# Twelve products of a zero tile ahead of the first transposes in a fused sliding-window attention and mixture-of-experts kernel

## The chip, the cores and the metric

The kernel runs on one core of one Trainium2 chip. The metric is the time of one execution on the device in microseconds (us), given as the median of several runs. The engines are named as the profile names them: PE is TensorE (PEld its weight loads), DVE is VectorE, ACT is ScalarE, POOL is GpSimd, SP is SyncE.

## The reference

Attention in a causal window of 64 positions over 8 batches, 8 heads, 576 positions and 64 channels a head; then the mean over the positions of a batch chooses one of eight experts for the whole batch, and that expert's two layers are applied.

```python
scores = (q @ k^T) / sqrt(64)                       # (8, 8, 576, 576)
mask   = (0 <= i - j) and (i - j < 64)
x      = softmax(where(mask, scores, -1e9)) @ v     # heads side by side: (8, 576, 512)
pooled = x.mean(axis=1)
logits = pooled @ w_gate                            # (8, 8)
e      = argmax(logits);  gate = softmax(logits)[e]
out[b] = gate[b] * (relu(x[b] @ w1[e[b]]) @ w2[e[b]])   # 512 -> 1024 -> 512
```

## The kernel before, in words

A batch is cut into five units: four for two heads each (512 positions), and one for the last 64 positions of all eight heads. The units are numbered through, so unit 0 to 4 are batch 0, 5 to 9 batch 1. For each unit PE transposes q and k (`T`, L225; L232 for the tail unit), ACT or DVE copy the transposes out of PSUM (`k` for the k half, L252, `U` for the q half, L242), PE makes the scores (`S`, L275, for some units with a mask product ahead, L269), ACT takes the exponential (`E`, L288 and L291), DVE or the mask product applies the band (`K`, L297), PE sums the rows by a product with ones (`l`, L309) and multiplies with v (`A`, L331), ACT makes the reciprocal as a logarithm and an exponential (`n`, L351, and `R`, L357), and DVE scales and adds up for the gate (`X`, L364). Before a batch's v can be used, DVE shifts half of it across the partitions (`V`, L150 and L151). When all five units of a batch are through, the gate is worked out (`g j G H I`), POOL reads the chosen expert's number (`P`), and the expert's weights are loaded by that number (`W`, L423 and L426). The experts' products (`c`, L461, L470, L503, L512) follow, mixed with the attention of later batches.

Nothing here is ordered by a scheduler. The table `OPS` at the head of the file is a list of such steps, and each engine gets its instructions in the order of that list and takes them strictly one after the other. An `m` in a step's name puts its result into one of the three buffers `mo` of the PSUM pool `ps_m`, in turn. Loads of q, k (`Q`, L110), the tail rows (`t`, L133), v (`L`, L141 and L145) and weights are issued by POOL; two loads at the start (`Y`, L119) are issued by SP in float32 and cast on DVE (`Cd`, L128).

The list already has a rule for a step `F` that the table before doesn't use, and the tile `warm` of zeros that `F` reads is cleared by DVE's first instruction (L168):

```python
elif c == "F":
    wps = ps_m.tile([128, 512], FP32, tag="mo", name="wps")
    for _ in range(int(x)):
        nc.tensor.matmul(out=wps, lhsT=warm[:, 0:128], rhs=warm, start=True, stop=True)
```

The table's beginning is the loads of batch 0 (`Y0.24 Q0.48 Q1.48 Q0.2 ...`), the casts, and then the transposes of batch 0 in the order unit 3, 2, 0, 1 (`Tm3 Tm2 T0 Tm1`), the scores of unit 3 (`Sb3`), and so on. On PE the transposes of unit 3 are the first work of the program.

Of the kernel before, what the change touches and what calls it, by code (L numbers as in the profile page):

```python
# [1 line left out]
OPS = (  # L2
    "Y0.24 Q0.48 Q1.48 Q0.2 Cd0.24 y i Q1.2 Y1.24 Q3 Cd1.24 z Tm3 Tm2 mb T0 Tm1 ka3 ka2 ka0 "
    "t0 Ud3 Ud2 Q2 Sb3 L0 L3 ka1 L1 L2 E3 Smb2 L4 Ud0 l3 Ud1 t1 S0 T4 E2 kd4 Ud4 n3 Smb1 E0 "
    "Mb K0 E1 R3 Q4 L9 Tm5 Sb4 Tm7 Tm8 Ud5 Q5 ka5 kd8 E4 L5 kd7 l1 n1 T6 l4 n4 Ud7 l2 Sb5 ka6 "
    "n2 R1 R4 l0 V0 A3 Ud6 L7 Am1 n0 E5 T9 X3 Am2 Ud9 S7 R2 L8 E7 Ud8 X1 R0 l5 X2 L6 n5 Smb6 "
    "A0 Am4 K7 ka9 E6 t2 X4 X0 Sb8 l7 g0 n7 T12 j0 Q6 Sm9 Tm10 G0 Ud12 kd12 E8 Ud10 H0 E9 "
    "Tm13 Tm11 R7 K9 l6 R5 ka10 Sb12 Ud11 ka13 V1 n6 Q7 l8 P0 Ud13 W0 I0 kd11 T14 Am5 A7 X7 "
    "A6 Ud14 kd14 L12 n8 X5 E12 R6 l12 n12 Sm14 X6 S11 l9 E14 Smb10 Tm17 E11 n9 T18 W1 Ud17 "
    "A9 W2 E10 S13 kd18 Ud18 L13 Tm15 Ud15 l10 Am8 R8 W3 kd15 ka17 T16 K14 L11 c X8 L14 n10 "  # L10
    "E13 R9 c ra X9 c R10 c rd c g1 K11 rd S17 j1 G1 ra ra c H1 L10 c rd l14 K13 c t3 ra c P1 "
    "n14 Q8 ra c c rd c V2 Ua16 c c ra ka16 l11 A10 X10 Am12 W4 c Q9 R12 X12 n11 ra W5 R11 "
    "A11 rd W6 T19 E17 c l13 n13 R13 Ua19 I1 X11 c Sm18 S15 K17 L15 rd E18 W7 R14 A13 c l17 "
    "ra X13 A14 c L16 L17 X14 g2 n17 Tm20 E15 ra kd19 c Ud20 ra L18 kd20 T22 S19 Sm16 E19 L19 "
    "j2 G2 c P2 t4 K15 E16 Q10 K18 c ra c W8 H2 ra ka22 c ra c c S20 l18 ra rd rd K16 c n18 "
    "Q11 K19 L21 ra Tm21 c c Ua21 Ud22 l16 W9 T23 R17 kd21 L23 V3 c c R18 c ra Am17 Ud23 n16 "
    "ra l15 E20 X17 L22 c R16 ka23 c rd n15 A18 c S23 X18 Sm21 K20 T24 kd24 ra R15 E21 L20 "
    "A16 c l19 L29 ra L24 W10 n19 Ud24 Am15 X16 A19 W11 R19 c X15 l20 E23 n20 L25 I2 c X19 rd "
    "L26 ra Tm26 c g3 K23 kd26 l23 Ud26 R20 c ra Sm22 n23 S24 j3 rd G3 E24 E22 T28 H3 K21 c "
    "Tm27 Ud28 P3 t5 ka27 kd28 l21 L28 rd n21 I3 K24 S26 L27 T25 c V4 W12 c Ua27 ra l24 c K22 "  # L20
    "c ra ra ra Ud25 n24 c R23 Q13 Q12 Am20 X20 R21 c c c rd Am23 W13 kd25 E26 A21 T29 rd X23 "
    "l22 Sm27 W14 W15 n22 E27 S28 V5 c c K26 K27 L32 c R24 l26 c X21 t6 A24 E28 Am22 ra R22 "
    "L30 ra K28 n26 X24 Ud29 kd29 c A27 l27 n27 c X22 ra ra c g4 S25 R26 rd Sm29 j4 G4 L34 "
    "E29 T32 Tm30 kd30 E25 Ud30 c Ua32 H4 K29 P4 ka32 ra c l28 R27 T33 L33 rd Ua33 S30 I4 n28 "
    "c Q15 c ra L31 ra Am26 ka33 c E30 c ra W16 X27 X26 ra l29 c K25 R28 c rd n29 Q14 A28 K30 "
    "c W17 X28 T34 S32 Sm33 ra O O E32 c E33 c K32 l25 n25 R25 c kd34 Am25 A29 W18 c O Ua34 "
    "R29 rd W19 T31 l30 c X29 X25 rd ka31 g5 c c Ud31 O ra K33 rd Sm31 n30 S34 j5 G5 c V6 R30 "
    "P5 rd O E31 H5 c K31 T36 l32 Ud36 rd E34 c t7 c A30 c n32 I5 rd L39 ka36 ra R32 l33 T35 "
    "X30 A32 Ua35 L38 rd c K34 rd c ka35 c n33 T37 ra Sm35 S36 L37 O E35 rd c X32 ra E36 W20 "
    "l34 c L35 n34 c K35 K36 L36 c kd37 R33 c O l31 rd W21 R34 rd c n31 R31 c Ua37 Tm38 O W23 "  # L30
    "Ud38 A33 ra ka38 Am34 l35 T39 X33 c n35 W22 c ra X34 A31 X31 g6 kd39 c O Sm38 R35 O S37 "
    "ra E38 j6 c c G6 P6 Ud39 E37 ra ra c V7 K38 rd H6 c l36 c K37 W24 n36 S39 A35 l37 ra rd "
    "E39 c ra n37 c X35 R36 c A37 c ra l38 Am36 K39 ra c c O R37 rd X37 n38 Am39 X36 O c rd c "
    "I6 l39 W27 R38 c n39 O O A38 rd R39 c W25 W26 ra X39 X38 g7 c j7 O c G7 c ra c P7 rd ra "
    "c c O W29 O c ra c O rd H7 O ra c O c W28 W31 ra O ra O c ra c c ra rd c c c c rd c W30 "
    "I7 O ra O c rd c c ra rd O c O O rd c O rd O O c rd c c O ra c c rd c O rd ra rd c c O "
    "rd O c c ra O O c c c c ra rd o O c ra O c ra o "
).split()

# [554 lines left out]
```

## Time and profile before

| | |
|---|---|
| median of 3 runs | 203.21 us |
| lowest and highest | 202.68 and 203.79 us |
| span of the profiled execution | 201.9 us, from its first to its last instruction |
| PE busy | 183.5 us (91% of the span) |
| ACT, DVE, POOL busy | 131.8, 119.9 and 111.0 us |
| bytes moved by DMA | 41.16 MB, mean 204 GB/s |

The span leaves out what lies around the first and the last instruction. Which of the three runs the profile was taken in isn't recorded; the span is 0.8 to 1.9 us below them, and 1.3 us below their median. "L225" is a line of the kernel before; in the changed kernel the table is one line shorter, so every line has a number lower by one there.

### The profile page before, as it was taken

How to read it: one execution, taken by the hardware profiler on the slowest of the kernel's cores; microseconds unless marked ns; L12 is line 12 of the kernel's file. 1: busy time of each engine (PE TensorE's matmuls, PEld its weight loads, DVE VectorE, ACT ScalarE, POOL GpSimd, SP SyncE). 2: the span in 40 equal slices, each digit the busy share in tenths (PEclk: the TensorE clock that was granted, in tenths of full speed). 3: DMA queues.
4: the chain of work that ended last, by engine and by line, in shares of the span. 5: the costliest groups of instructions: out<-in, count | busy, mean ns of one | idle time of the engine just before them, and what ended most of it. 6: DMA issues, size and time to landing. Idle time of an engine off the chain costs nothing.

```text
span 201.9 us, 8105 instructions
## 1 busy us (share of the span) xinstructions
PE 183.5 (91%) x3518; PEld 124.2 (62%) x3522; DVE 119.9 (59%) x347; ACT 131.8 (65%) x247; POOL 111.0 (55%) x158
## 2 busy tenths in 40 slices
PE   0487886899999999999999999999999999999991
PEld 0455564656677756577667666676656666776760
DVE  3527989595477546895877457966494651216410
ACT  2179998876599578977779975757787436321121
POOL 7985939235931593478633552439452716553561
PEclk9999999999999999999999999999999999999998
DMA  6999999999999999999999999999999999999693
GB/s 135 175 188 159 194 162 198 199 198 174 196 201 197 170 198 193 174 201 167 200 206 200 169 195 223 259 208 137 183 237 243 266 254 212 274 212 301 235 325 134
DMA packets 83346, 41.16 MB, mean 204 GB/s; under 512 B 48080, under 2 KB 80976, under 8 KB 83312
## 3 DMA queue, kind: packets, MB, share of 16 engines
q0 software_dynamic: 81936, 39.72, 138.5%
q1 hardware_dynamic: 768, 0.85, 1.3%
q8 instruction: 27, 0.44, 0.8%
q10 hardware_dynamic: 608, 0.08, 0.2%
q14 instruction: 7, 0.06, 0.1%
HBM read 61.88 MB, written 9.44 MB: 353 GB/s over the span
## 4 chain that ended last, share of the span: by engine, by line
PE 77%; DMA 9%; POOL 7%; issue 3%; DVE 2%; ACT 1%; POOLq 0%; DVEq 0%; ACTq 0%
PE ph L461 28%; PE po L503 25%; DMA vw<-in_v_dram 9%; PE tp L225 5%; PE ph L470 4%; PE s L275 4%; PE av L331 3%; PE po L512 3%; PE lb L309 3%; POOL vw L141 2%; POOL km L110 2%; POOL qm L110 1%; POOL out_dram L492 1%; PE gps L392 1%; POOL qkt L133 1%
## 5 line engine op out<-in xcount | busy, mean ns | idle before, releaser
L503 PE MATMUL po<-w2b,hm 128*64 128x512 f16 x512 | 60.1, 379 | 0.0
L461 PE MATMUL ph<-xm,w1b 128*64 128x512 f16 x512 | 60.0, 379 | 0.0
L461 PEld LDWEIGHTS <-w1b 128*64 128x64 f16 x512 | 31.7, 110 | 18.7 <-issue 0.4
L503 PEld LDWEIGHTS <-hm 128*64 128x64 f16 x512 | 30.1, 110 | 19.3
L141 POOL DMA_DIRECT2D vw<-in_v_dram x32 | 28.9, 910 | 13.3 <-DMA w1b<-in_moe_w_dram 4.3
L446 ACT ACTIVATE hm<-ph,gw 128x512 f16<-128x512 f32 x39 | 26.6, 693 | 13.4 <-PE ph L461 13.3
L492 POOL DMA_DIRECT2D out_dram<-ob x31 | 17.2, 557 | 25.0 <-DMA w1b<-in_moe_w_dram 7.0
L351 ACT ACTIVATE ln<-lb 128x512 f32<-128x512 f32 (+1 forms) x40 | 22.5, 563 | 11.8 <-PE lb L309 8.6
L364 DVE CUSTOM_DVE_ANT_0 xm<-av,rl 128x512 f16<-128x512 f32 x32 | 21.6, 686 | 10.4 <-PE av L331 9.5
L482 ACT COPY ob<-po 128x512 f32<-128x512 f32 x18 | 10.6, 586 | 23.6 <-PE po L503 23.6
L448 DVE TENSOR_SCALAR hm<-ph,gw 128x512 f16<-128x512 f32 x25 | 18.7, 748 | 12.1 <-PE ph L461 11.6
L357 ACT ACTIVATE rl<-ln 128x512 f32<-128x512 f32 (+1 forms) x40 | 23.3, 594 | 1.5 <-DVE pool L364 1.3
L225 PE MATMUL tp<-ident,qm 128*64 128x128 bf16 x256 | 13.8, 232 | 7.4 <-DMA qm<-in_q_dram 6.9
L288 ACT ACTIVATE pe<-s 128x1024 f16<-128x1024 f32 x19 | 19.5, 1028 | 1.4 <-PE s L275 0.7
L297 DVE TENSOR_TENSOR pe<-pe,mask 128x1024 f16<-128x1024 f16 x24 | 16.3, 687 | 3.9 <-ACT pe L288 3.1
L252 ACT COPY kT<-tp 128x512 bf16<-128x512 bf16 x19 | 11.2, 597 | 9.0 <-PE tp L225 8.0
L225 PEld LDWEIGHTS <-qm 128*64 128x64 bf16 x256 | 10.7, 118 | 10.0 <-DMA qm<-in_q_dram 6.9
L482 DVE COPY ob<-po 128x512 f32<-128x512 f32 x14 | 9.7, 690 | 10.7 <-PE po L503 10.5
L423 POOL DMA_DIRECT2D w1b<-in_moe_w_dram x16 | 12.6, 785 | 5.9 <-DMA vw<-in_v_dram 2.9
L275 PEld LDWEIGHTS <-kT 64*128 64x128 bf16 x576 | 10.1, 95 | 8.9 <-issue 5.6
L331 PEld LDWEIGHTS <-vw 128*64 128x64 f16 x512 | 12.4, 112 | 4.7 <-issue 1.2
L225 PE MATMUL tp<-ident,km 128*64 128x128 bf16 x256 | 13.9, 231 | 1.4 <-DMA km<-in_k_dram 0.9
(80 smaller groups left out, 267.2 us busy)
## 6 DMA issues: line engine op xcount, KB each, us to landing
w1b<-in_moe_w_dram POOLq DMA_DIRECT2D x16, 512.0 KB, 9.3
w2b<-in_moe_w_dram POOLq DMA_DIRECT2D x16, 512.0 KB, 13.4
out_dram<-ob POOLq DMA_DIRECT2D x31, 256.0 KB, 8.1
vw<-in_v_dram POOLq DMA_DIRECT2D x32, 128.0 KB, 9.0
km<-in_k_dram POOLq DMA_DIRECT2D x7, 512.0 KB, 9.3
qm<-in_q_dram POOLq DMA_DIRECT2D x7, 512.0 KB, 9.0
out_dram<-obt POOLq DMA_DIRECT2D x14, 64.0 KB, 7.7
qkt<-in_q_dram POOLq DMA_DIRECT2D x8, 64.0 KB, 7.6
```

Of the source, the lines that this page charges most:

```text
L141: nc.gpsimd.dma_start(out=vt[:, 2 * J + 1], in_=v[b, :, 128 * J:128 * J + 128].rearrange("h c d -> c h d"))
L225: nc.tensor.transpose(tp[p0:p0 + 64, n, r], t[:, 2 * i + hh, ts(r, 64)], ident)
L288: nc.scalar.activation(out=po, in_=sp[0], func=AF.Exp, scale=scale)
L351: nc.scalar.activation(out=ln, in_=lb[:, 0:n], func=AF.Ln)
L357: nc.scalar.activation(out=rl, in_=lns.pop((b, i)), func=AF.Exp, scale=-1.0)
L364: nc.vector.tensor_tensor_reduce(out=xm[:, i], in0=av.rearrange("q r p -> q (r p)"), in1=rl, scale=1.0, scalar=0.0, op0=ALU.mult, op1=ALU.add,
L446: nc.scalar.activation(out=o, in_=i, func=AF.Relu, scale=g)
L448: nc.vector.tensor_scalar(out=o, in0=i, scalar1=g, scalar2=0.0, op0=ALU.mult, op1=ALU.max)
L461: nc.tensor.matmul(out=ph[64 * c:64 * c + 64], lhsT=w1t[:, kb, ts(2 * ft + c, 64)], rhs=xm[:, kb], start=(kb == 0), stop=(kb == 3), skip_g ...
L482: copy(e)(out=ob, in_=po)
L492: (nc.scalar if n and eng is nc.sync else eng).dma_start(out=dst, in_=src)
L503: nc.tensor.matmul(out=po[64 * c:64 * c + 64], lhsT=hm[:, fb, ts(2 * r + c, 64)], rhs=w2t[:, fb], start=(fb == 0), stop=(fb == 7), skip_gr ...
```

## The change

One word is put at the head of the table, and the rest of the table is only broken into lines differently. PE gets 24 instructions more (twelve weight loads and twelve products of 128x128 by 128x512 zeros, all into one PSUM buffer) ahead of the first transposes. The products are read by nobody. They take one of the three `mo` buffers first, so that every later user of that pool gets the next buffer in turn.

```diff
 OPS = (
-    "Y0.24 Q0.48 Q1.48 Q0.2 Cd0.24 y i Q1.2 Y1.24 Q3 Cd1.24 z Tm3 Tm2 mb T0 Tm1 ka3 ka2 ka0 "
+    "F12 Y0.24 Q0.48 Q1.48 Q0.2 Cd0.24 y i Q1.2 Y1.24 Q3 Cd1.24 z Tm3 Tm2 mb T0 Tm1 ka3 ka2 ka0 "
...
```

The head of PE's queue before: `qm` is the q of batch 0 in SBUF, `tp` the PSUM tile of unit 3's transposes.

```order
L589 UNCONDITIONAL_BRANCH [waits barrier_Pool_Activation_PE_DVE_SP_release]
L225 LDWEIGHTS qm_126 [waits DMASW0_49]
L225 MATMUL tp_146<-ident_105,qm_126 64x128 [waits Pool_49]
```

And now, where ten further pairs like the one shown stand at the line of dots; `warm` is the zero tile, `wps` the buffer that the products go to:

```order
L588 UNCONDITIONAL_BRANCH [waits barrier_Pool_Activation_PE_DVE_SP_release]
L548 LDWEIGHTS warm_110 [waits DVE_49]
L548 MATMUL wps_124<-warm_110 128x512
...
L224 LDWEIGHTS qm_139 [waits DMASW0_49]
L224 MATMUL tp_159<-ident_105,qm_139 64x128 [waits Pool_49]
```

The first transposes still wait for the load of q and for POOL's identity, and now stand behind the products, which wait for DVE's clearing of `warm`. The second place is unit 1's transposes on PE, before:

```order
L225 MATMUL tp_184<-ident_105,km_128 64x128
L225 LDWEIGHTS qm_126 [waits DVE_49]
L225 MATMUL tp_201<-ident_105,qm_126 64x128
```

and now:

```order
L224 MATMUL tp_197<-ident_105,km_141 64x128
L224 LDWEIGHTS qm_139 [waits DVE_49]
L224 MATMUL tp_214<-ident_105,qm_139 64x128 [waits PE_49]
```

Unit 1 is the third to take an `mo` buffer before, and the fourth now; it gets the buffer of the zero products and so has a wait for PE's own earlier work. DVE, ACT, POOL and SP have the same instructions in the same order with the same waits as before, and so has PE outside these two places.

67 rows, old and new, of the table OPS are left out of this document.

## The prediction

> **What bounds the kernel now.** I read the page first, then busy time by stage, then the chain that ended last in order of time, then PE's first instructions one by one.
>
> ```profile
> span 201.9 us, 8105 instructions
> ```
>
> The busy times by stage (us, then busy time of PE, PEld, DVE, ACT, POOL with counts, granted clock, DMA share, GB/s):
>
> ```profile
> 12.50:22.26 9.76, 7.88 (x181) 5.03 (x183) 5.87 (x13) 8.82 (x17) 6.93 (x9) 1.00 1.94 176
> 22.26:31.32 9.06, 7.53 (x210) 5.43 (x212) 7.64 (x32) 8.88 (x19) 5.73 (x8) 1.00 1.95 176
> ...
> 41.00:197.60 156.60, 156.50 (x2838) 104.57 (x2832) 94.15 (x268) 101.97 (x193) 80.94 (x115) 1.00 1.40 213
> ```
>
> From 41 us on PE has no gaps (156.50 of 156.60), so the end is the moment at which PE gets there plus a fixed amount of PE work. Everything turns on the first 41 us, where PE waits. What it waits for there, the chain in order of time says (start, duration, what):
>
> ```profile
> 9.54 9.13 DMA vw<-in_v_dram
> ...
> 18.96 0.89 POOL km L110
> 19.84 2.83 POOL vw L141 x3
> 22.68 8.52 DMA vw<-in_v_dram
> ...
> 31.32 0.88 DVE vw L150
> ...
> 34.09 0.60 DVE xm L364
> ...
> 34.75 0.44 PE av L331 x16
> ...
> 38.18 0.50 issue
> ...
> 41.01 4.32 PE ph L461 x40
> ```
>
> PE first appears at 34.75, and the experts' products begin at 41.01. Before that the chain is a load of batch 0's v that must land before POOL may issue more, the issues and the loads of batch 1's v, and then DVE's shift of that v and what is queued behind it on DVE. None of these steps waits for PE.
>
> **The change, part by part.** First what the change could save. PE's early instructions (start, duration, and in brackets idle time before and what ended it):
>
> ```profile
> 6.88 0.64 PE L225 MATMUL tp<-ident,qm 128*64 128x128 bf16 x8 [6.88 <-DMA qm<-in_q_dram]
> 8.41 0.64 PE L225 MATMUL tp<-ident,km 128*64 128x128 bf16 x8 [0.89 <-DMA km<-in_k_dram]
> 8.83 0.64 PE L225 MATMUL tp<-ident,qm 128*64 128x128 bf16 x8
> ...
> 10.97 0.64 PE L225 MATMUL tp<-ident,km 128*64 128x128 bf16 x8
> 11.54 0.61 PE L269 MATMUL s<-maskb,ident 128*128 128x512 bf16 x1
> ...
> 12.86 0.60 PE L269 MATMUL s<-maskb,ident 128*128 128x512 bf16 x2
> ...
> 17.30 0.39 PE L225 MATMUL tp<-ident,km 128*64 128x128 bf16 x8
> 17.53 0.39 PE L225 MATMUL tp<-ident,qm 128*64 128x128 bf16 x8
> ...
> 20.72 0.38 PE L269 MATMUL s<-maskb,ident 128*128 128x512 bf16 x1 [0.16 <-issue]
> ```
>
> Until about 12.5 us PE runs at half speed: from 8.83 to 10.97 five groups of eight transposes take 2.14 us, 0.43 a group, where at 17.30 a group takes 0.23; the same 128x512 mask product takes 0.61 at 11.54 and 0.38 at 20.72. At 12.86 two of them take 0.60 together, which is full speed already. The column of the granted clock reads 1.00 throughout, so the clock's state must be read here from durations. The products of zeros would put this slow stretch into the idle time ahead of 6.88.
>
> *Their own cost.* They wait for DVE's first instruction:
>
> ```profile
> 1.05 0.27 DVE L168 MEMSET warm<- 128x256 uint32 x1 [1.05 <-PEq L578]
> ```
>
> That is done at 1.32; I start them at 1.4. A 128x512 product lasts 0.61 at half speed and 0.38 at full, 0.23 less; if half speed doubles the spacing from one product to the next, that spacing is 0.23 at full and 0.46 at half speed. The transposes, two at a time and 128 wide, give 0.43 / 4 x 4 = 0.43 for the same 512 columns. I take 0.43: 12 x 0.43 = 5.2, done by 6.6, ahead of q's arrival at 6.88: cost nothing. At worst each takes its full 0.61 with no overlap: 12 x 0.61 = 7.3, done at 8.7. Then unit 3's transposes start late, but all 64 at the fast pace (8 x 0.23 = 1.84) end at 10.5 against 11.4 (10.97 + 0.43) before: still no loss. The added wait in unit 1 is for PE's own finished products and costs nothing; queued behind it is all the rest of PE's work, but it comes after 48 transposes, when the products are long done.
>
> *What it saves at the place.* Before, unbroken work began at 8.41, and the clock rose between 11.97 (11.54 + 0.43, where unit 3's second mask product begins) and 12.86: 3.6 to 4.5 us later. From 1.4 that is 5.0 to 5.9, so the clock is up before 8.41. From 8.41, seven groups at 0.23 in place of 0.43 save 1.4 us, and the two mask products of unit 3 another 0.46: 1.86. Part of it is lost at once, to a load of k for heads 0 and 1 (issue on POOL, and the row of its landing: KB, us from issue to landing):
>
> ```profile
> 4.75 1.63 POOL L110 DMA_DIRECT2D km<-in_k_dram  x2
> km<-in_k_dram POOLq DMA_DIRECT2D x1, 128.0 KB, 4.9
> ```
>
> It lands at 4.75 + 4.9 = 9.65, and unit 0's k transposes would be due at 8.41 + 4 x 0.23 = 9.33: 0.3 lost. So the first scores, and with them the first exponential on ACT, come 1.5 us earlier:
>
> ```profile
> 12.97 1.02 ACT L288 ACTIVATE pe<-s 128x1024 f16<-128x1024 f32 x1 [0.73 <-PE s L275]
> ...
> 19.72 0.38 ACT L351 ACTIVATE ln<-lb 128x256 f32<-128x256 f32 x1 [0.39 <-PE lb L314]
> ```
>
> The start at 12.97 becomes about 11.4.
>
> *Where it goes.* Three later places don't move, since they wait for loads whose issue on POOL has nothing to do with PE:
>
> ```profile
> 7.79 0.90 POOL L110 DMA_DIRECT2D qm<-in_q_dram  x1
> qm<-in_q_dram POOLq DMA_DIRECT2D x1, 512.0 KB, 8.0
> ...
> 15.94 0.41 PE L225 MATMUL tp<-ident,qm 128*64 128x128 bf16 x8
> ...
> 20.34 0.89 DVE L150 COPY vw<-vw 64x2048 f16<-64x2048 f16 x1 [0.54 <-DMA vw<-in_v_dram]
> 22.26 0.63 PE L331 MATMUL av<-pe,vw 128*64 128x64 f16 x28 [0.42 <-DVE vw L151]
> 30.76 0.42 DVE L242 COPY qt<-tp 128x512 bf16<-128x512 bf16 x1 [0.30 <-PE tp L225]
> ```
>
> First, batch 1's q lands at 7.79 + 8.0 = 15.79, and PE now begins its transposes at 15.94, behind the scores of batch 0. PE comes there 1.5 us earlier, waits, and everything behind in its queue is ahead by 0.15 us. ACT, which from 12.97 to the gap ahead of 19.72 was behind its orders, has worked off its backlog by then, and the row sums and logarithms around 20, where PE and ACT take turns, come some 0.4 us earlier (the size of ACT's gap at 19.72 is my measure for that). Second, DVE's shift of batch 0's v already waited 0.54 us for its load at 20.34, and PE's products with v waited for the shift at 22.26: both stay where they are, and what is left is ACT's lead of 0.4. It goes through the rest of batch 0 to its gate and to the issue of its weights. Third, batch 1's v lands at 22.68 + 8.52 = 31.20, and DVE, which ends its copy before it at 30.76 + 0.42 = 31.18, starts the shift at 31.32. DVE earlier by 0.4 waits for the landing instead: at best the shift starts 0.1 earlier. Behind it DVE has no gap up to 34.69, and PE's next product with v stands on that (34.75). So of the 1.5 us, 1.35 end at 15.94, the 0.4 that ACT wins back end at 31.32, and at 34.75 the kernel is 0 to 0.1 us earlier; I take 0.1. What PE has to do from there is unchanged. 24 more instructions shift where PE's code is fetched; the 0.5 us at 38.18 that the chain puts down to "issue" is my bound for that, 0.5 either way. So the cost of the whole change lies between 1.86 gained and, with the worst rival below, 1.4 lost.
>
> The sum against the profiled span: 201.9 - 0.1 = 201.8, and against the median 203.21 - 0.1 = 203.1.
>
> **The rivals.**
>
> *The lead is carried.* If the landing at 31.20 moves with the rest, or DVE's shift is not what PE's product at 34.75 stands on, PE's lead of 1.5 us lives. It can't be worth more than 1.86, and the chunk at 41 needs its weights: first half issued at 30.04, landing 9.4 us after it.
>
> ```profile
> 30.04 0.75 POOL L423 DMA_DIRECT2D w1b<-in_moe_w_dram  x1 [1.34 <-DVE kT L252]
> w1b<-in_moe_w_dram POOLq DMA_DIRECT2D x1, 512.0 KB, 9.4
> ```
>
> That is 39.4, a margin of 1.6 to the start at 41.01. I take 1.2, so that something of the 1.5 is lost to other loads: 202.0 us. For it: a changed pace of DVE could shift POOL's issues and with them landings that come of a chain of issues. Against it: three waits for loads in a row, the last with 0.14 us of slack.
>
> *The clock falls back.* The twelve products end at 6.6 or sooner, and the next products that aren't transposes are the masks at about 10.1. If transposes don't hold the clock, PE is again at half speed when the scores come, and stays so in the stretch 12.5 to 22.26, which it crosses with pauses while it waits for loads. The end of the program shows how long the clock holds without work:
>
> ```profile
> 180.00:201.90 21.90, 17.61 (x234) 12.58 (x230) 6.42 (x10) 4.09 (x7) 8.63 (x16) 0.96 0.81 252
> 196.54 1.07 PE L512 MATMUL po<-w2b,ht 128*64 128x256 f16 x16
> ```
>
> A mean of 0.96 over 21.9 us means half speed for some 1.75 us, from 200.1, that is 2.5 us after PE's last product ends (197.61). From 6.6 to 10.1 is 3.5 us, longer than that. The price, from PE's work in the stretch 12.5 to 22.26 (count, then busy us, mean ns):
>
> ```profile
> L309 PE MATMUL lb<-pe,ones 128*64 128x512 f16 x8 | 1.6, 390 | 0.7 <-ACT ln L351 0.5 <-ACT pe L288 0.2
> L269 PE MATMUL s<-maskb,ident 128*128 128x512 bf16 x5 | 1.6, 383 | 0.2 <-issue 0.2
> L225 PE MATMUL tp<-ident,km 128*64 128x128 bf16 x32 | 1.6, 219 | 0.0
> ```
>
> With q's there are 64 transposes, eight groups at 0.20 more; five mask products and four pairs of row sums at 0.23 more: 1.6 + 2.1 = 3.7. Less the idle 1.9 of that stretch and the lead of 1.5 this is 0.3 at 22.26. The next stretch, with 1.5 idle and no lead, would lose 3.7 - 1.5 = 2.2 if the clock stayed down through it; I take half: 0.3 + 1.1 = 1.4, 204.6 us. The deciding point is whether eight transposes a group count as work. The Trainium skill, "TensorE: Matmul & The Clock Gate", Part 4, says that they don't count as busy in the same way and that full speed doesn't engage for them, which would give this rival's time. Against it stands the trace: the clock rose at about 12.5 after 3.1 us of transposes and only 0.9 us of other products, and held through the groups at 17.30 and 17.53.
>
> *It doesn't do what it says.* The clock isn't up by 8.41, because its window falls badly or zeros don't count: 203.2 us, as before.
>
> **How the numbers follow.** About 0.5% (1.0 us) is what a measurement of this kernel can tell from no change. Forecast, hidden behind the loads: 0.58, 203.1, its own range 202.5 to 203.8 (the 0.5 us of code fetch and the spread of runs). Carried: 0.23, 202.0. Falls back: 0.13, 204.6. Does nothing: 0.06, 203.2. Faster by over 0.5% is the carried case, 0.23; slower the fallen clock, 0.13; the two others, 0.64, lie within. The range of 201.7 to 204.5 takes in most of the carried case and cuts the upper half of the slow one, so that no more than 2 in 10 is left out.
>
> **What would show it.** Right: groups of eight transposes at 0.23 from 8.41, the first exponential near 11.4, PE waiting for a load ahead of batch 1's transposes at 15.8, a longer wait of DVE for v at 20.3 and a new one at 31.2, PE's product with v within 0.1 of 34.75. Wrong: that product a microsecond earlier (the lead is carried), or durations of 0.6 for a mask product after 12.5 (the clock fell).

## The result and the profile after

| | before | changed |
|---|---|---|
| median | 203.53 us (15 runs, 202.68 to 204.46) | 204.45 us (15 runs, 203.64 to 206.27) |
| profiled execution | span 201.9 | time 204.17, span 202.6 |
| ratio | | 1.0063, 95% interval 1.0042 to 1.0085 |

The change makes the kernel slower, by 0.6% in the ratio and by 0.9 us between the medians, where I had forecast no change. In the experiments below every ratio is to runs of the kernel before on the same chip. One profile there, that of the kernel with batch 1's q moved ahead, is of a disturbed run, and only the place of a wait is read from it.

The page of the changed kernel gives the span, with 24 instructions more than before:

```profile
span 202.6 us, 8129 instructions
```

The busy times by stage (us, then PE, PEld, DVE, ACT, POOL with counts, granted clock, DMA share, GB/s):

```profile
8.41:12.50 4.09, 3.73 (x74) 3.03 (x74) 1.27 (x3) 2.34 (x4) 3.83 (x5) 0.58 1.62 183
12.50:22.26 9.76, 7.50 (x165) 4.63 (x165) 5.75 (x12) 8.65 (x16) 7.42 (x10) 1.00 1.92 175
...
41.00:197.60 156.60, 156.47 (x2844) 105.46 (x2840) 94.88 (x268) 102.03 (x193) 80.51 (x115) 1.00 1.39 212
```

From 41 us on PE is as full as before (156.47 of 156.60, before 156.50). But in the first row the clock is 0.58: PE was at half speed in most of the stretch that the products were to have made fast. The early rows say when (start, duration, what, idle time before and its end):

```profile
1.38 4.67 PE L548 MATMUL wps<-warm 128*128 128x512 bf16 x12 [1.38 <-DVE warm L167]
...
6.95 0.41 PE L224 MATMUL tp<-ident,qm 128*64 128x128 bf16 x8 [0.90 <-DMA qm<-in_q_dram]
...
8.53 0.49 PE L224 MATMUL tp<-ident,qm 128*64 128x128 bf16 x8
8.81 0.64 PE L224 MATMUL tp<-ident,km 128*64 128x128 bf16 x8
9.24 0.64 PE L224 MATMUL tp<-ident,qm 128*64 128x128 bf16 x8
...
12.51 1.02 ACT L287 ACTIVATE pe<-s 128x1024 f16<-128x1024 f32 x1 [0.73 <-PE s L274]
```

The products run from 1.38 to 6.05, and groups are fast at 6.95 and 8.29. Then the spacing is 0.43 again (8.81 to 9.24). By the trace's record of the granted clock it rose at 5.3, fell at 8.7 and rose again at 12.1 (before: once, at 12.57). The first exponential starts at 12.51, only 0.46 ahead of before. Further on:

```profile
16.66 0.41 PE L224 MATMUL tp<-ident,qm 128*64 128x128 bf16 x8 [1.10 <-DMA qm<-in_q_dram]
...
22.65 0.63 PE L330 MATMUL av<-pe,vw 128*64 128x64 f16 x28 [0.43 <-DVE vw L150]
...
31.15 0.42 DVE L241 COPY qt<-tp 128x512 bf16<-128x512 bf16 x1 [0.31 <-PE tp L224]
31.61 0.97 DVE L149 COPY vw<-vw 64x2048 f16<-64x2048 f16 x1
...
35.14 0.44 PE L330 MATMUL av<-pe,vw 128*64 128x64 f16 x16 [1.08 <-DVE pool L363]
```

Batch 1's transposes start at 16.66 instead of 15.94, after a wait of 1.10 us for q; the products with v at 22.65 instead of 22.26; PE's place in the chain at 35.14 instead of 34.75. The shift of batch 1's v (31.61, before 31.32) doesn't wait for its load here: it follows a copy that waits for PE's transposes, so PE's lateness goes through. The issue of that q, and the row of its landing:

```profile
7.83 0.90 POOL L109 DMA_DIRECT2D qm<-in_q_dram  x1
qm<-in_q_dram POOLq DMA_DIRECT2D x1, 512.0 KB, 8.8
```

It is issued 0.04 us later than before and takes 8.8 us instead of 8.0. So PE is 0.39 us late at 22 us. The rest comes late: set against the same instructions of before, PE's weight loads are 0.41 us late from 40 to 85 us, 0.48 at 95, 0.65 from 125 to the end.

### The profile page after: what moved, and what is told of

It is laid out like the page before. It is cut to its first block, busy times and chain, and to the rows that moved or that the text cites. A ratio compares the mean times of both kernels' runs of the same rounds, so it can differ in the third digit from the quotient of the medians.

```text
span 202.6 us, 8129 instructions
## 1 busy us (share of the span) xinstructions
PE 187.7 (93%) x3530; PEld 126.2 (62%) x3534; DVE 120.5 (60%) x347; ACT 132.0 (65%) x247; POOL 110.9 (55%) x158
## 4 chain that ended last, share of the span: by engine, by line
PE 66%; DMA 13%; POOL 6%; issue 5%; DVE 4%; ACT 3%; POOLq 1%; DVEq 0%; ACTq 0%
PE ph L460 21%; PE po L502 20%; PE tp L224 6%; DMA w2b<-in_moe_w_dram 5%; DMA w1b<-in_moe_w_dram 5%; DMA qm<-in_q_dram 4%; PE s L274 4%; PE av L330 4%; PE ph L469 3%; PE lb L308 3%; POOL out_dram L491 3%; PE po L511 2%; DVE xm L363 1%; POOL km L109 1%; ACT ln L350 1%
## 5 line engine op out<-in xcount | busy, mean ns | idle before, releaser
L502 PEld LDWEIGHTS <-hm 128*64 128x64 f16 x512 | 31.2, 110 | 18.7 <-issue 0.3
L350 ACT ACTIVATE ln<-lb 128x512 f32<-128x512 f32 (+1 forms) x40 | 22.4, 561 | 12.5 <-PE lb L308 9.2
L447 DVE TENSOR_SCALAR hm<-ph,gw 128x512 f16<-128x512 f32 x25 | 18.7, 748 | 12.1 <-PE ph L460 11.6
L422 POOL DMA_DIRECT2D w1b<-in_moe_w_dram x16 | 12.5, 779 | 6.1 <-DVE kT L251 2.3
L241 DVE COPY qt<-tp 128x512 bf16<-128x512 bf16 x25 | 10.4, 417 | 9.0 <-PE tp L224 5.1
```

The costliest lines, as they stand in the source:

```text
L350: nc.scalar.activation(out=ln, in_=lb[:, 0:n], func=AF.Ln)
L502: nc.tensor.matmul(out=po[64 * c:64 * c + 64], lhsT=hm[:, fb, ts(2 * r + c, 64)], rhs=w2t[:, fb], start=(fb == 0), stop=(fb == 7), skip_gr ...
```

## The experiments

Four theories stand in the expectations. A, B and C come from comparing the two traces and from the first runs; D was formed after the eighth run.

- **A, an early code load.** PE's code comes by DMA in blocks of 16,384 bytes. The 24 added instructions bring the first such load ahead of the landing of batch 1's q, which then lands some 0.8 us later.
- **B, the products' work**, or the clock's fall after it.
- **C, the lead turns idle.** PE, early, waits ahead of batch 1's transposes, and the clock falls in that wait.
- **D, block ends.** PE stands still at every 256th instruction until the next block is there. Added instructions move the block ends to other places of the program, and where a block has gone by quickly, in short instructions, the wait is longer.

The code loads are rows of the DMA queue "instruction" in short windows, 14.0 to 15.2 us of the changed kernel first, then 16.2 to 17.0 us of the kernel before (packets, MB, share):

```profile
q8 instruction: 1, 0.02, 5.0%
```

```profile
q8 instruction: 1, 0.02, 7.5%
```

Both kernels have 27 such loads. The first starts at 14.53 in the changed kernel and at 16.44 before, where it comes behind the landing of q (7.79 + 8.0 = 15.8).

### Work or count: twelve empty products, six, eighteen

`n12_narrow` keeps the count and takes the work away:

```diff
-nc.tensor.matmul(out=wps, lhsT=warm[:, 0:128], rhs=warm, start=True, stop=True)
+nc.tensor.matmul(out=wps[:, 0:64], lhsT=warm[:, 0:128], rhs=warm[:, 0:64], start=True, stop=True)
```

> The twelve products are kept, but 64 columns wide in place of 512, so that PE gets the same 24 instructions and almost no work from them. Theory A (code load): the 24 instructions move PE's first code load (16,384 bytes on one DMA engine, at 16.44 us before and at 14.53 in the changed kernel) ahead of the landing of batch 1's q, which then lands 0.8 us later; so here too the code load comes near 14.5, batch 1's transposes start near 16.6 (15.94 before, 16.66 changed), and the time is like the changed kernel's, 0.3 to 0.7% above before. Theory B (the products' work or the clock's fall that follows it): no work and no early clock here, so the time is as before within 0.15%, and batch 1's transposes start at 15.9.

Measured: 204.69 us, ratio 1.0048 (1.0022 to 1.0075). The loss is there without the work, which can't be its main part. In its profile, the slowest of the twelve runs, the first code load comes at 14.77, and PE waits for q:

```profile
16.86 0.42 PE L224 MATMUL tp<-ident,qm 128*64 128x128 bf16 x8 [1.94 <-DMA qm<-in_q_dram]
```

That is as A has it; but the clock, up at 10.32, also fell from 17.14 to 20.56, as C has it. How much the fall takes can be read from the runs' mean granted clock: 3.4 us at half speed make 0.992 of a span of 203 us. Seven of the twelve runs have 0.997 or more, so no such fall, and their median is 204.34, where before's runs of 0.996 or more have 203.67: most of the loss is there without it.

`f6` and `f18` change the number alone:

```diff
-    "F12 Y0.24 ...
+    "F6 Y0.24 ...
```

> Six wide products in place of twelve: 12 instructions, work from 1.4 to about 4.0 us. Theory A: all or nothing, by whether the code load is asked for ahead of PE's wait for batch 1's q: near 14.5 us and +0.3 to 0.7%, or near 16.4 us and the time as before. Theory B: about half of the excess, +0.3%, wherever the code load is.

Measured: 204.12 us, 1.0041 (1.0013 to 1.0069). The first code load comes at 15.77, between A's two cases and ahead of q, which lands at 16.5 (7.85 + 8.7).

```diff
-    "F12 Y0.24 ...
+    "F18 Y0.24 ...
```

> Eighteen products: PE works past 6.9 us, so that the stretch in which the clock fell in the changed kernel (5.4 to 8.8 us, mostly idle) is mostly filled. Both theories expect the clock to hold: groups of eight transposes at 0.23 us from 8.3, first exponential near 11.2. Theory A: the code load is early all the same, batch 1's transposes start near 16.6, and the time stays 0.3 to 0.7% above before. Theory B (the clock's fall costs): at least as fast as before.

Measured: 206.56 us, 1.0133 (1.0097 to 1.0168), the largest loss so far. In this profile the early clock held, so that PE came to batch 1's transposes still earlier, and waited (12 to 21.5 us):

```profile
16.41 0.41 PE L224 MATMUL tp<-ident,qm 128*64 128x128 bf16 x8 [1.92 <-DMA qm<-in_q_dram]
...
17.63 0.64 PE L224 MATMUL tp<-ident,qm 128*64 128x128 bf16 x8
18.05 0.64 PE L224 MATMUL tp<-ident,km 128*64 128x128 bf16 x8
```

After 1.92 us of idle time the groups are at 0.42 again: the clock fell at 17.33, as C has it.

### Batch 1's q issued earlier

```diff
-    "t0 Ud3 Ud2 Q2 Sb3 ...
+    "Q2 t0 Ud3 Ud2 Sb3 ...
```

> The changed kernel, with the load of batch 1's q issued on POOL ahead of batch 0's tail rows (near 6.4 us in place of 7.8). Theory A: even with the code load on top it lands by about 15.2, PE is no longer late at batch 1's transposes (15.5 in place of 16.66), the 0.39 us at PE's later product with v goes, and the time is 0.2 to 0.4% below the changed kernel's, near before. Theory B: no change against the changed kernel, +0.6%.

Measured: 207.33 us, 1.0162 (1.0121 to 1.0204): a miss. The 512 KB went ahead of the small load of the tail rows, on which PE stands next:

```profile
17.51 0.64 PE L231 MATMUL tpt<-ident,qkt 128*64 128x128 bf16 x8 [2.05 <-DMA qkt<-in_k_dram]
```

It says nothing of A or C, since it made a wait of its own.

### The wait filled, or taken by other work

`f18_fill` puts eight products into the wait that `f18` showed, `f12_fill` four into that of the changed kernel:

```diff
-    "F12 Y0.24 ...
+    "F18 Y0.24 ...
...
-    "K0 E1 R3 Q4 L9 Tm5 ...
+    "K0 E1 R3 Q4 L9 F8 Tm5 ...
```

> Eighteen products at the start, and eight more directly ahead of batch 1's transposes, where PE idled 1.92 us in the kernel with eighteen alone (14.49 to 16.41) and the clock fell from 17.33 to 20.74. Theory C (the lead becomes an idle stretch ahead of that late load, and the clock falls in it): with the stretch filled the clock holds, groups of eight transposes stay at 0.23 us through 20, and the median goes from 206.56 to 204.5 or less. Theory A alone (only the late load costs): the load lands as late as before (16.4), the time stays near 206.5.

Measured: 207.03 us, 1.0133 (1.0096 to 1.0171). The fill did its work, and the time didn't follow (12 to 23 us):

```profile
14.68 1.90 PE L548 MATMUL wps<-warm 128*128 128x512 bf16 x8
16.51 0.41 PE L224 MATMUL tp<-ident,qm 128*64 128x128 bf16 x8
...
18.32 0.39 PE L224 MATMUL tp<-ident,km 128*64 128x128 bf16 x8
...
22.44 0.63 PE L330 MATMUL av<-pe,vw 128*64 128x64 f16 x28 [0.37 <-DVE vw L150]
```

No idle time ahead of 16.51, groups at the fast pace, and the products with v only 0.18 us later than before. Yet the kernel ends 3.3 us later than before by the medians. So the wait ahead of batch 1's transposes is not the main cause, and the main loss of this kernel comes behind 22 us, where PE has the same work as before. In this profile the clock fell later, at 39.07 for 3.4 us; but five of the six runs have a granted clock of 0.996 or more, and took 205.81 to 207.44 us all the same.

```diff
-    "K0 E1 R3 Q4 L9 Tm5 ...
+    "K0 E1 R3 Q4 L9 F4 Tm5 ...
```

> The changed kernel with four more products directly ahead of batch 1's transposes, where its profile shows PE idle for 1.10 us (15.56 to 16.66). Theory C: fewer executions with a fallen clock, so the runs above 205 us go and the median falls from 204.45 by 0.3 to 0.6. Theory A alone: as the changed kernel, 204.4, or a little more for eight more instructions.

Measured: 205.44 us, 1.0072 (1.0047 to 1.0097), no better than the changed kernel: a miss. (One of ten runs took 380.04 us, which I can't explain; it doesn't move the median.)

`f12_s4first` lets the tail unit's scores go ahead of batch 1's transposes:

```diff
-    "K0 E1 R3 Q4 L9 Tm5 Sb4 Tm7 ...
+    "K0 E1 R3 Q4 L9 Sb4 Tm5 Tm7 ...
```

> The changed kernel with the scores of batch 0's tail unit ahead of batch 1's first transposes on PE instead of behind them: useful work of about 0.6 us (16.51 to 17.06 before) in the stretch where PE waits for the late load. Theories A and C: PE is 0.4 to 0.6 us further along after the transposes, the 0.39 us at 34.75 goes, and the time is 203.4 to 204.0. If the loss were not at this place (theory B, the products' work), no change: 204.4.

Measured: 204.38 us, 1.0025 (1.0002 to 1.0048): a smaller loss than the changed kernel's, though the intervals overlap, and not as small as A and C gave. Four of the twelve runs, of a granted clock of 0.997 or more, took 203.67 to 204.00, which is before's time; the eight others, of 0.992 or less, took 204.25 to 205.41. In this kernel the loss goes with a fallen clock. In its profile the scores stand in front of the late load:

```profile
17.41 0.38 PE L268 MATMUL s<-masktb,ident 128*128 128x256 bf16 x2 [0.41 <-ACT pe L287]
...
17.94 0.41 PE L224 MATMUL tp<-ident,qm 128*64 128x128 bf16 x8
```

`n3_narrow` has three empty products, six instructions:

```diff
-    "F12 Y0.24 ...
+    "F3 Y0.24 ...
...
-nc.tensor.matmul(out=wps, lhsT=warm[:, 0:128], rhs=warm, start=True, stop=True)
+nc.tensor.matmul(out=wps[:, 0:64], lhsT=warm[:, 0:128], rhs=warm[:, 0:64], start=True, stop=True)
```

> Three narrow products (64 columns): six more instructions than before and next to no work. Theory A: the code load comes at 15.5 to 16.4 us and, if it is behind the landing of batch 1's q (15.8), time as before within 0.2%; if ahead, 0.3 to 0.5% above. Theory B and C: as before within 0.2%.

Measured: 203.97 us, 1.0001 (0.998 to 1.0021): no change.

### What D came from: the loss in steps

PE's weight loads, each set against the same one of the kernel before (mean lateness in us over the 5 us from the time named; the added products are left out), show where each profiled execution loses its time. The last four are there for comparison; `n3_narrow` and `b_again`, a second execution of the kernel before, show how far one profile can be off:

| kernel | added | 20 us | 45 us | 90 us | 110 us | 125 us | 195 us |
|---|---|---|---|---|---|---|---|
| changed | 24 | +0.39 | +0.41 | +0.28 | +0.48 | +0.64 | +0.65 |
| n18_narrow | 36 | +0.64 | +1.06 | +1.17 | +1.36 | +2.06 | +2.06 |
| n26_narrow | 52 | +0.11 | +1.65 | +1.91 | +1.99 | +3.14 | +3.15 |
| f18_fill | 52 | +0.19 | +2.41 | +2.39 | +3.15 | +4.32 | +4.91 |
| t116 | 232 | +0.42 | +2.48 | +2.43 | +2.43 | +2.52 | +2.52 |
| t128 | 256 | -0.46 | -0.42 | -0.38 | +0.19 | +0.19 | +0.18 |
| n12_narrow | 24 | +1.76 | +1.88 | +2.00 | +1.99 | +2.38 | +2.38 |
| f18 | 36 | +1.18 | +1.54 | +1.91 | +1.90 | +2.54 | +2.55 |
| n3_narrow | 6 | +0.92 | +0.76 | +0.62 | +0.84 | +0.84 | +1.01 |
| b_again | 0 | -0.06 | +0.15 | +0.01 | +0.21 | +0.21 | +0.99 |

In the changed kernel PE is 0.45 us early at 14 us and 0.72 late at 16, behind batch 1's q. After 20 us the lateness is flat for tens of microseconds and jumps at a few moments. Counted from the program's first weight load, with the added products, PE's semaphore instructions and one product for each weight load (most of the traces lack four records), PE stops behind instruction 1,215, and in one profile or another behind 1,471, 1,727, 2,238, 3,519, 4,543 and 6,079, which lie multiples of 256 further on (within 1), whatever instruction stands there. The first of these is what the prediction quoted as 0.50 of "issue" at 38.18. In the kernel before, the changed one and the one with 52 empty instructions it is this:

```profile
37.96 0.22 PE L225 MATMUL tp<-ident,km 128*64 128x128 bf16 x1
38.68 0.38 PE L225 MATMUL tp<-ident,km 128*64 128x128 bf16 x7 [0.50 <-issue]
```

```profile
37.90 0.33 PE L224 MATMUL tp<-ident,km 128*64 128x128 bf16 x5
38.76 0.27 PE L224 MATMUL tp<-ident,km 128*64 128x128 bf16 x3 [0.53 <-issue]
```

```profile
37.06 0.40 PE L274 MATMUL s<-qt,kT 64*128 64x64 bf16 x15
38.71 0.19 PE L274 MATMUL s<-qt,kT 64*128 64x64 bf16 x1 [1.25 <-issue]
...
119.98 0.40 PE L502 MATMUL po<-w2b,hm 128*64 128x512 f16 x1
121.17 1.05 PE L502 MATMUL po<-w2b,hm 128*64 128x512 f16 x8 [0.79 <-issue]
```

The break comes in the midst of a unit's eight transposes or sixteen scores, where nothing of the program waits. In the changed kernel it comes behind the fifth transpose, where before it came behind the first. With 52 instructions it falls into the scores, and is 1.25 us instead of 0.5. From one weight load to the next, this break is 0.77 before, 0.80 in the changed kernel, 0.94 in `f18` and `n18_narrow`, 1.57 in `n26_narrow`, 1.58 in `f18_fill`; the one at 120 us is 0.21, 0.39, 0.87, 0.92, 1.19 and 1.21.

What PE waits for there, the queue "instruction" shows: each of these breaks of over 0.5 us ends 1.2 to 1.6 us after the end of a load of 16,384 bytes; the loads are some 6 us apart. Before, the load ran from 36.23 to 37.17 and PE went on at 38.68; in `n26_narrow` 36.24 to 37.19 and 38.83, and near 120 us 118.90 to 119.79 and 121.17. That the break grows where the block goes by quickly fits the end near 120 us: 6.0 us for the block and a break of 0.21 before, 4.9 and 0.39 in the changed kernel, 4.3 and 0.9 with 36 instructions, 3.8 and 1.2 with 52. It doesn't fit the end near 38 us: 5.4 us and 0.77 before, 6.7 and 1.57 in `n26_narrow`; nor does it fit `t96`, with 5.1 and 1.27 near 117 us.

### D put to the test

Empty products alone, 18 and 26 of them, as in `n12_narrow`:

```diff
-    "F12 Y0.24 ...
+    "F18 Y0.24 ...
...
-nc.tensor.matmul(out=wps, lhsT=warm[:, 0:128], rhs=warm, start=True, stop=True)
+nc.tensor.matmul(out=wps[:, 0:64], lhsT=warm[:, 0:128], rhs=warm[:, 0:64], start=True, stop=True)
```

> Eighteen narrow products (64 columns): the instruction count of the kernel with eighteen wide ones (36 more than before), nearly none of its work. Theory D (every 16,384 bytes of PE's code, 256 instructions, PE stands still until the next block is there; the added instructions move all blocks against the program, and the wait grows where a block now ends behind short instructions): the stalls stay at the same row numbers as with eighteen wide ones, near 37, 51 and 120 us, and the time is 205.5 to 206.8, as there (206.56). Theories B and C (work, clock): near 204.

Measured: 205.56 us, 1.0083 (1.0052 to 1.0114), with breaks of 0.94 near 38, 0.45 near 51 and 0.92 near 120 us.

```diff
-    "F12 Y0.24 ...
+    "F26 Y0.24 ...
...
-nc.tensor.matmul(out=wps, lhsT=warm[:, 0:128], rhs=warm, start=True, stop=True)
+nc.tensor.matmul(out=wps[:, 0:64], lhsT=warm[:, 0:128], rhs=warm[:, 0:64], start=True, stop=True)
```

> Twenty-six narrow products, the count of the kernel with eighteen and eight (52 more instructions). Theory D: stalls of about a microsecond near 37, 95 and 121 us as there, time 206 to 207.5 (207.03 there). Theories B and C: near 204.

Measured: 206.67 us, 1.0131 (1.0092 to 1.0171), beside 1.0133 of `f18_fill`, which has the same count with all the work. The breaks come near 37 (1.57), 44 (0.99) and 120 us (1.19), none near 95. `n18_narrow` against `f18` (1.0133) leaves 0.5%, 1.0 us, that may be C's fallen clock; their intervals overlap.

`t128` adds a whole block, 256 instructions, so that all later block ends fall on the instructions on which they fell before:

```diff
-    "F12 Y0.24 ...
+    "F128 Y0.24 ...
...
-nc.tensor.matmul(out=wps, lhsT=warm[:, 0:128], rhs=warm, start=True, stop=True)
+nc.tensor.matmul(out=wps[0:64, 0:48], lhsT=warm[:, 0:64], rhs=warm[:, 0:48], start=True, stop=True)
```

> 128 tiny products (64 columns of weights, 48 wide) in place of twelve wide ones: 256 instructions, exactly one block of PE's code, so that every block but the first ends at the same place of the program as before the change. PE is busy from 1.4 to about 6.5 us as with the twelve. Theory D: the stalls are those of before, time within 0.25% of before (203.7). If added instructions cost by their number: far above 207. Theories B and C: as the changed kernel, 204.4.

Measured: 203.75 us, 1.0006 (0.9979 to 1.0033): no loss from ten times as many added instructions. They end 2 us after the change's (8.06, the change's at 6.05) and warm PE too, and the clock, up at 7.58, didn't fall again, so that PE is 0.46 us ahead at 20 us: part of the difference from the changed kernel is this early lead (first two rows; the others are DVE's shift of batch 1's v, and PE's product in the chain):

```profile
1.38 6.68 PE L548 MATMUL wps<-warm 128*64 128x48 bf16 x126 [1.38 <-DVE warm L167]
...
9.04 0.39 PE L224 MATMUL tp<-ident,km 128*64 128x128 bf16 x8
...
30.86 0.90 DVE L149 COPY vw<-vw 64x2048 f16<-64x2048 f16 x1
...
34.32 0.44 PE L330 MATMUL av<-pe,vw 128*64 128x64 f16 x16 [1.08 <-DVE pool L363]
```

`f12_t116` puts 116 tiny products behind the twelve wide ones, 256 instructions in all:

```diff
                 nc.tensor.matmul(out=wps, lhsT=warm[:, 0:128], rhs=warm, start=True, stop=True)
+            for _ in range(116):
+                nc.tensor.matmul(out=wps[0:64, 0:48], lhsT=warm[:, 0:64], rhs=warm[:, 0:48], start=True, stop=True)
```

> The changed kernel with all of its twelve products, and 116 tiny ones behind them, so that 256 instructions are added, one block of code. PE's extra work lasts to 9 or 10 us, so the first transposes start late, at full clock. Theory D: the blocks end where they did before, and the loss goes: time within 0.3% of before (203.7) although the products are all there. Theories B and C: 204.4 or more, since work is only added.

Measured: 206.46 us, 1.0102 (1.0064 to 1.0139): a miss, with the same whole block added as in `t128`. The tiny products held unit 3's transposes until 10.41 instead of 6.88, and with PE late and no longer waiting for loads, it stood still for over a microsecond at two early block ends where `t128` loses nothing:

```profile
10.41 0.24 PE L224 MATMUL tp<-ident,qm 128*64 128x128 bf16 x1
...
15.38 0.24 PE L274 MATMUL s<-qt,kT 64*128 64x64 bf16 x5 [1.24 <-issue]
...
28.69 0.22 PE L330 MATMUL av<-pe,vw 128*64 128x64 f16 x2 [1.42 <-issue]
```

`t116` and `t96` are `t128` with 232 and 192 instructions, 24 and 64 short of a block:

```diff
-    "F128 Y0.24 ...
+    "F116 Y0.24 ...
```

> 116 tiny products: 232 instructions, 24 short of a block, so that the blocks move by 24 instructions the other way from the change. Theory D: other waits, none of them grown like those at 95 and 120 in the changed kernel; if the waits grow steadily with the shift they now shrink, and with the clock up early the time is 203.0 to 203.7, at or below before. Theories B and C: as with 128 (203.75).

```diff
-    "F128 Y0.24 ...
+    "F96 Y0.24 ...
```

> 96 tiny products: 192 instructions, 64 short of a block. Theory D gives no sign for so far a shift, only that the waits stand at the same row numbers and the time follows their sum: 203 to 206. Theories B and C: as with 128 (203.75).

Measured: 206.07 us, 1.0121 (1.0083 to 1.0159), and 206.05 us, 1.0108 (1.0074 to 1.0141). Fewer instructions of the same kind than in `t128` cost some 2 us more. In `t116` one break, at the same count of 1,215 and now amid batch 1's products with v, takes PE from 0.66 to 1.77 us late, and a fall of the clock from 37.82 to 41.23 behind it takes it to 2.48. The break (32 to 36 us):

```profile
33.50 0.23 PE L330 MATMUL av<-pe,vw 128*64 128x64 f16 x3
35.09 0.64 PE L330 MATMUL av<-pe,vw 128*64 128x64 f16 x29 [1.36 <-issue]
```

Last, a copy of each kernel for a second profile:

```diff
 (no edit: the changed kernel, and the kernel before)
```

> The changed kernel once more, for a second execution's profile. Theory D: PE stands still again at the rows that end a block of 256 instructions, with the longest waits near 38, 95 and 120 us, as in the first profile (0.80, 0.41 and 0.39 us from one weight load to the next), and the first code load comes near 14.5. If the losses at 95 and 120 were chance, they are elsewhere now.

> The kernel before once more, for a second execution's profile. Theory D: the first code load comes near 16.4 us again, the wait near 38 is 0.77 again, and those near 95 and 120 are the 0.2 us of an ordinary step.

Measured: 204.10 and 204.49 us, spans 202.5 and 202.9. The copy of the changed kernel is 0.63 late at 20 us and 0.60 at the end; its break near 38 is 0.79 again and that near 120 is 0.32, but that near 95 is an ordinary 0.21. The copy of before has its first code load at 16.40 and 0.77 near 38; it is 0.06 early at 20 us, 0.21 late at 110 (a break of 0.61 near 108, in the first profile 0.21), and then loses 0.8 at a load near 150 us that the other profiles don't wait for. One profile can be off by as much as the effect.

**What is settled.** The products' work isn't the loss (`n12_narrow` loses without it, `n26_narrow` as much as `f18_fill`), and neither is the number of added instructions by itself (`t128` against `t116` and `t96`). For 36 and 52 instructions the profiles of `n18_narrow` and `n26_narrow`, in which the clock didn't fall between its rise and the end of PE's work, show most of the loss at block ends (1.4 of 2.1 us and 3.0 of 3.2 us come behind 20 us), and each such break ends with a load of code. That the place of the block ends alone decides is not shown: `f12_t116` has them where `t128` has them, and loses 1%.

**What is open.** With 24 instructions, block ends explain only 0 to 0.25 us of the 0.65 and 0.60 in the two profiles; 0.39 and 0.63 are there by 20 us, behind the late q. A would explain that: q took 8.8 and 9.0 us in the two profiles of the changed kernel, 9.0 in `n12_narrow`, 8.0 and 8.6 in those of before. But `b_again` shows 8.6 with its first code load at 16.40, where q is landing (7.86 + 8.6), `n3_narrow` shows 9.6 with it at 17.47, and `t128` only 8.1 with code loads at 7.76 and 15.22, both while q was under way. A is argued, not shown, and these speak against it; it was never taken away alone. A fallen clock goes with part of the loss: the eleven runs of the changed kernel of a granted clock of 0.992 or less have a median of 205.06 us, the four of 0.998 or more 204.40, still 0.9 above before's 203.53. So why these 24 instructions cost 0.9 us stays open in the main.

## Why the prediction was wrong

1. *"Their own cost"*: right. The products start at 1.38 (1.4 expected) and end at 6.05 (6.6 expected), ahead of q, and cost nothing by their work.
2. *"The clock is up before 8.41"*: up at 5.3, but it fell again at 8.7. I had let it rise and hold. Between 5.3 and 8.7 PE had the end of the products and three groups of transposes, with waits for loads between. The profiles of `a_again`, `f12_fill` and `f12_s4first`, with the same twelve products, show it too: up at 6.15 to 6.84, down again 3.4 us later. So the first exponential came at 12.51, not 11.4, and in the second profile of the changed kernel at 13.16, later than before (12.97, and 12.64 in `b_again`). This is the rival "the clock falls back" in its condition, not in its reason: in `t128` the clock stayed up from 7.58 although PE had nearly nothing but transposes until 10.89 (9.04 row). Its price, half speed through 12.5 to 22.26, did not come: the mean there is 1.00.
3. *"Three later places don't move, since they wait for loads whose issue on POOL has nothing to do with PE"*: the step that failed. For q the issue didn't move (7.83), the landing did, by 0.8 us, and PE, forecast to stay in time at 22.26, came 0.39 late (22.65). For batch 1's v the issue moved too: POOL itself waits for landings (1.24 us at 18.96 before), and began it at 19.32 instead of 19.83, so this load no longer held anything back. I had taken the time from issue to landing as a constant of the trace, from one execution, and had asked only what PE's lead could do to DVE and ACT, not what else could change a transfer.
4. *"That is my bound for that, 0.5 either way"*: a term right for this change, but of the wrong kind. I saw the code fetch, but took it for one row that might shift. A load comes for every 256 instructions. The largest single waits measured 1.2 to 1.6 us, and the sum for 52 instructions was 3 us. For the 24 of this change it was 0 to 0.25, within the 0.5, so this is not what made the forecast fail. I had also counted it as of either sign and so as nothing in the middle; of eight counts of added instructions tried (6 to 232, a whole block left out) none gained, one was even and seven lost.
5. *"DVE earlier by 0.4 waits for the landing instead"*: not borne out either. In `t128` the shift of batch 1's v began at 30.86 instead of 31.32, and its product in the chain at 34.32, 0.43 ahead of before. The landing moves with what stands before it (POOL began the issue at 19.13 there), as the rival "the lead is carried" had it; the lead was then lost at the block ends near 96 and 108 us, where the breaks were 0.62 and 0.56 instead of 0.19 and 0.21. These ends fall on the instructions on which they fell before, so a break varies at one and the same place too.

## What to carry to other kernels

An instruction added to a queue that is full to the end has two prices: its work, and its place in the count; in the kernels with 36 and 52 more instructions the second was paid up to some 100 us later, at block ends that fell behind other instructions than before. Before a change is judged by its sign, run it once with its added instructions emptied: if the empty one costs the same, the idea isn't what was measured. Filling the count up to a whole block is no sure test: it took the loss away in `t128` and not in `f12_t116`. And a time from issue to landing in one profile is a sample, not a constant: a forecast that pins three places to it needs its spread.

## What the runs showed of the hardware that I had not expected

PE's code arrives in loads of 16,384 bytes, 27 in this program and 28 with 52 instructions more. PE can stand still where a multiple of 256 instructions ends, for up to 1.6 us, until 1.2 to 1.6 us after the end of such a load; at most of these ends it doesn't. The Trainium skill, "Runtime: NRT & Kernel Launch", section "Instruction fetch mechanics", has the 16 KiB blocks of 256 instructions and calls the cost of crossing a boundary mostly hidden; the first part agrees with these traces, the second not always (idle 1.25 us ahead of 38.71 in `n26_narrow`, 1.36 ahead of 35.09 in `t116`).

The clock fell after short idle times: at 8.7 with the products ended at 6.05 and three groups of transposes since, and in `f18` at 17.33 after a single gap of 1.92 us. The Trainium skill, "TensorE: Matmul & The Clock Gate", Part 1, has free-running windows of 3.4 us, and the changes at 5.3, 8.7 and 12.1 are that far apart; but it warns of gaps longer than such a window, and 1.92 us was enough here. Part 4 of that page says that full speed doesn't engage for transposes; in `t128` groups of eight ran 0.22 to 0.25 us apart (8.57 to 9.27), with a clock that tiny products had raised at 7.58.
